# Attention start-up on one core: filler matmuls between the first heads' row scores, with clears and transposes reordered

## The chip, the cores and the metric

The kernel runs on one core of one Trainium2 chip. The metric is the device time of one execution in microseconds, the median of several runs; lower is better.

## The reference

32 heads of causal attention (4 batches of 8 heads, 576 positions, 64 columns per head) with a bias made of a running sum, and then two gated networks.

```python
scores = scale * np.matmul(q, k.transpose(0, 1, 3, 2))
cum = np.cumsum(np.maximum(s, 0.0), axis=-1)
bias = -(cum[:, :, :, None] - cum[:, :, None, :])
scores = np.where(causal, -1000000000.0, scores + np.minimum(bias, 0.0))
attn = np.exp(scores - np.max(scores, axis=-1, keepdims=True))
attn = attn / (np.sum(attn, axis=-1, keepdims=True) + 1e-09)
x = np.matmul(attn, v)            # then (2304, 512)
x = (1 / (1 + np.exp(-(x @ w_gate))) * (x @ w_val)) @ w_out
out = ((x @ w_a) * (x @ w_b)) @ w2_out
```

## The kernel before

The attention part takes the first fifth of the time and the two networks the rest. Everything is recorded as operations with a name, an engine, dependencies and a priority number. In the attention part a list scheduler (`emit(in_order=True)`) takes, among the operations whose dependencies have been taken, the one with the lowest number; so the numbers set the order of the instructions on each engine's queue, and each queue is then worked off strictly in that order, with semaphores between the engines. A transfer is issued by SP's, ACT's or GpSimd's queue and counts as an instruction of it.

One head i goes through these operations; the names are used below.

- `lqk` (L380, SP) loads the head's q and k. `hq1`, `hk1` (L532, L533, ACT) round them into the operand tile `o` (four of these tiles, used in turn; rows 0 to 63 are q and k, the rows behind hold the bias).
- The bias rows of `o` are filled by transfers: `sel` (L435 and L436, SP: two constant pieces), `rel` (L542, SP, from head 3 on), `relk` (L500 on SP for heads 0 to 2, L543 on GpSimd from head 3 on), and `relq` (L476, several queues, heads 0 to 2). Rows 64 to 127 of each `o` tile have to be cleared before: tile 0 at L390 (VectorE), tiles 1 and 2 by `ms` (L488, GpSimd), tile 3 by the first line of `more` (L399, VectorE).
- `S(i,0)` and `S(i,1)` (L557 and L562, TensorE) are the row scores in two halves, three matmuls and then one or two bf16 products that add the causal mask from `mkb` through the unit matrix `idb`. `mx(i,0)`, `mx(i,1)` (L570, VectorE) take their row maxima.
- `mT(i)` (L577, TensorE) transposes the maxima, `mc` (L579, ACT) copies them, `md` (L581, ACT's queue) sends them into `o`.
- `hk2`, `hq2` (L534, L535) send the rounded halves across, and `lok`, `loq` (L536, L538) take the low parts.
- `ST(i)` (L594 and L595, TensorE) are the transposed scores; they need `md(i)`, `lok(i)` and `loq(i)`. Then come the exponentials (L600, ACT), the causal clears (L616, GpSimd) and, by pairs of heads, the products with the values (L641) and the sums (L654).

`busy` (L410) is a run of products that nobody reads, TensorE's first work, 40 of them; it needs `mkb`, which ACT makes from GpSimd's `masks`. `more` clears tile 3 of `o` and eight small pieces of other tiles. The row scores of the first heads share one accumulator tile `g` for S(i,0): S(i+1,0) has to wait until mx(i,0) has read it.

The first of the networks' weight loads (L194, SP, 512 KB) stands on SP's queue between `rel(3)` and `sel(3)`:

```python
op(("more"), "DVE", 2.2, more, [], -149)
op(("rel", i), "SP", 0.5, lambda: ..., relst + done, t0 - 3 * HT + 0.05, lat=2.2)
```

A wait that follows from two writes of the same place is put in by the tile framework, in the order in which the operations are recorded, whether or not it is in an operation's list of dependencies.

Of the kernel before, what the change touches and what calls it, by code (L numbers as in the profile page):

```python
# [12 lines left out]
ALU = mybir.AluOpType  # L13
# [9 lines left out]
def f32(ap):  # L23
    return ap.bitcast(FP32)


class Schedule:
# [92 lines left out]
def attn_mlp_kernel(  # L120
# [14 lines left out]
    nc = tc.nc  # L135
# [3 lines left out]
    D = vt.shape[-1]  # L139
# [193 lines left out]
    def attention():  # L333
        with ExitStack() as c2:
# [16 lines left out]
            KB = R1 + 2  # L351
# [3 lines left out]
            CQ1, CK1 = 0, 640  # L355
# [6 lines left out]
            dn = tile1([128, QD], FP32, "dn")  # L362
# [4 lines left out]
            idb = tile1([128, 128], BF16, "idb")  # L367
            mkb = tile1([128, 448], BF16, "mkb")
# [3 lines left out]
            o_t = [tile1([128, CK1 + S], F32R, f"o{i}") for i in range(NO)]  # L372
            p_t = [tile1([128, 2 * S], F32R, f"o2_{i}") for i in range(3)]
            rel = tile1([128, 2, S], F32R, "rel")
# [31 lines left out]
            def busy():  # L406

                ps = sc.get("F", "busy")
                for _ in range(NBUSY):
                    nc.tensor.matmul(out=ps[:, 0:256], lhsT=idb, rhs=mkb[:, 192:448], start=True, stop=True)  # L410

            def selector():

                nc.gpsimd.memset(sel, 1.0)
                nc.gpsimd.affine_select(sel, sel, [[1, S]], ALU.is_ge, 0.0, base=0, channel_multiplier=-SR)
                nc.gpsimd.affine_select(sel, sel, [[-1, S]], ALU.is_ge, 0.0, base=SR - 1, channel_multiplier=SR)
# [17 lines left out]
            def selectors(o):  # L434
# [3 lines left out]
            sc = Schedule({  # L438
                "g": [psum1("ps_g", 1024)],
                "E": [psum1("ps_e", 1024)],  # L440
                "F": [psum1("ps_f")],
                "t": [psum1("ps_t")],
                "px": [psum1("ps_x", 1024)],
                "raw": list(raw_t),
                "u": [0],
                "W": wslot[:2],
                "stg": stg,
            })
            op = sc.op
# [33 lines left out]

            op("s", "SP", 0.5, load_s, [], -300, lat=2.3)
            op("selc", "Pool", 1.9, selector, [], -300)
            op("masks", "Pool", 0.9, masks, ["selc"], -280)
            for j in range(1, 3):
                op(("ms", j), "Pool", 1.2, lambda j=j: nc.gpsimd.memset(f32(o_t[j][D:2 * D]), 0.0), ["masks"], -270)  # L488
            op("pads", "DVE", 0.6, pads, [], -249)
            op("more", "DVE", 2.2, more, [], -149)  # L490
            op("mkb", "ACT", 0.7, masks_b, ["masks"], -280)
            op("mkc", "ACT", 0.2, masks_c, ["mkb"], -279)
            op("busy", "PE", 8.0, busy, ["mkb"], -270, acq=("F", "busy"), rel=("F", "busy"))
# [5 lines left out]
            for i in range(3):  # L499
                op(("relk", i), "SP", 0.65, lambda i=i: nc.sync.dma_start(  # L500
                    out=f32(o_t[i][D:R1, CK1:CK1 + S]), in_=f32(rel[i:NR * BH:BH])), ["sums"] + [("ms", i)] * (i > 0), -210 + i, lat=2.2)
# [6 lines left out]
            relst = ["relz"] + [("rels", c) for c in range(NR)]  # L508

            HT = 6.1  # L510
            NBUSY = 40
            WLATE = HT

            def head(i):
                b, h = divmod(i, H)  # L520
                t0 = HT * i
                o, o2, r, pt = o_t[i % NO], p_t[i % 3], r_t[i % NR2], pt_t[i % NPT]
                nm, mr = nm_t[i % 4], mr_t[i % 3]
                k1, q1, k2, q2 = o[:, CK1:CK1 + S], o[:, CQ1:CQ1 + S], o2[:, S:2 * S], o2[:, 0:S]
                up, dn = slice(0, D), slice(D, 2 * D)
                done = [("ST", i - NO, c) for c in range(NC)] + [("S", i - NO, g) for g in range(2)]
                done2 = [("ST", i - 3, c) for c in range(NC)]

                if i >= NR2:
# [4 lines left out]
                op(("hk2", i), "ACT", 0.7, lambda: nc.scalar.dma_start(out=f32(k2[dn]), in_=f32(k1[up])), [("hk1", i)] + done2, (-209.8, -209.6, -8.55)[i] if i < NR2 else t0 - 2 * HT + 0.35)  # L534
                op(("hq2", i), "SP", 0.5, lambda: nc.sync.dma_start(out=f32(q2[up]), in_=f32(q1[up])), [("hq1", i)] + done2, (-208.5, -207.5, -206)[i] if i < NR2 else t0 - 2 * HT + 0.1)  # L535
                op(("lok", i), "DVE", 0.9, lambda: nc.vector.tensor_tensor(  # L536
                    out=k2[up], in0=r[dn], in1=f32(k2[dn]), op=ALU.subtract), [("hk2", i)], (-8.7, -8.3)[i] if i < 2 else t0 - HT - 0.3)
                op(("loq", i), "DVE" if i < 2 else "Pool", 0.9 if i < 2 else 1.4, lambda: (nc.vector if i < 2 else nc.gpsimd).tensor_tensor(  # L538
                    out=q2[dn], in0=r[up], in1=f32(q1[up]), op=ALU.subtract), [("hq1", i)] + done2, -151 + 2 * i if i < 2 else t0 - HT + 1.45)

# [7 lines left out]
                for g, cs in ((0, (3, 2, 0)), (1, (1, 4))):  # L548
# [26 lines left out]
                       first_at[g] if first_at and first_at[g] else t0 + (3.5 - 2 * HT, -HT)[g], acq=to)  # L575
                    op(("mx", i, g), "DVE", (1.4, 1.1)[g], maxima, [("S", i, g), ("mT", i - 4), "pads"], (first_at[g] or 6.1) + 0.05 if first_at else t0 + (4.3 - 2 * HT, 0.7 - HT)[g], rel=to)
                op(("mT", i), "PE", 0.15, lambda: nc.tensor.transpose(sc.get("t", ("m", i))[0:NC, 0:128], nm[:, 0:NC], idf),  # L577
                   [("mx", i, 0), ("mx", i, 1), "masks"], (-8.7, -8.4)[i] if i < 2 else t0 - HT + 3.4, acq=("t", ("m", i)))
                op(("mc", i), "ACT", 0.25, lambda: nc.scalar.copy(out=mr, in_=sc.get("t", ("m", i))[0:NC, 0:128]),  # L579
                   [("mT", i), ("md", i - 3)], (-8.7, -8.4)[i] + 0.05 if i < 2 else t0 - HT + 3.55, rel=("t", ("m", i)))  # L580
                op(("md", i), "ACT", 0.4, lambda: nc.scalar.dma_start(  # L581
                    out=f32(o[KB:KB + 1, CQ1:CQ1 + 640]), in_=f32(mr)), [("mc", i)] + done, (-8.7, -8.4)[i] + 0.06 if i < 2 else t0 - HT + (3.93, 5.21)[i % 2], lat=2.2)


                tiles = {0: ("E", (i, 0)), 1: ("E", (i, 0)), 2: ("F", (i, 0)), 3: ("F", (i, 0)), 4: ("t", ("p", i))}
# [109 lines left out]
            for e, (ld, ab, *dv) in enumerate(LOADS):  # L695
                n, m = e // 2, e % 2
                prio = HT * ld + (0.5 if e > 2 else 0)
                last = convert(sc, n, m, [("S", max(int(ld) - 1, 0), 0)], prio,
                               at=[HT * ab + 1.2 - prio] + [HT * dv[k] - 0.15 + y - prio for k, y in ((0, 0), (0, 0.01), (1, 0), (2, 0))])
# [8 lines left out]
            done = [("xd", j) for j in range(H)]  # L708
# [302 lines left out]
```

## Time and profile before

| what | value |
|---|---|
| median of 3 runs | 1040.98 us (1038.46 to 1041.43) |
| the profiled execution | 1043.03 us |
| its span | 1041.3 us, so 1.7 us lie around it |
| TensorE busy in the span | 1011.0 us, 97% |
| TensorE's granted clock over the span | 0.992 of full |

The span is the time between the first and the last instruction of the profiled execution. A busy TensorE is one that has a matmul in it, at whichever clock. The granted clock is 1.0 at 2.4 GHz and 0.5 at 1.2 GHz; before the first change that the profiler saw it is shown as 1.0.

### The profile page before, as it was taken

Reading aid. Unit: us, or ns where it says so; the run is one execution under the profiler, and the core shown is the slowest. Engines: PE = TensorE matmul, PEld = TensorE weight load, DVE = VectorE, ACT = ScalarE, POOL = GpSimd, SP = SyncE. Lnnn points to the kernel's source line nnn. Section 1 sums busy time; section 2 is a strip of 40 time slices with the busy share of each in tenths; the row PEclk is TensorE's granted clock in tenths of the full one; section 3 lists DMA queues with packets and bytes.
Section 4 is the critical chain, followed back from the end, with each engine's and each line's share of the span. In section 5 each row is a group of like instructions: output and inputs, shape, how many; then the busy total and the mean of one; then the engine's idle time right before and its main releaser. Section 6 shows DMA issues by size and latency. Waiting matters only on the chain.

```text
span 1041.3 us, 17117 instructions
## 1 busy us (share of the span) xinstructions
PE 1011.0 (97%) x6160; PEld 914.1 (88%) x6160; DVE 694.4 (67%) x1146; ACT 466.8 (45%) x891; POOL 388.1 (37%) x388
## 2 busy tenths in 40 slices
PE   6999999999999999999999999999999999999998
PEld 5777666789999999998888899999999999888886
DVE  7787778779689665669855238967876567933222
ACT  3566666655455444545334225343433333432221
POOL 5568687652366333433300013245532342400000
PEclk7999999999999999999999999999999999999999
DMA  5667777441243321446553442123432244544333
GB/s 147 172 160 200 206 206 170 129 147 58 101 131 111 128 99 69 145 159 231 178 171 109 122 128 83 59 102 127 128 109 94 92 153 160 196 138 133 111 107 101
DMA packets 93586, 139.76 MB, mean 134 GB/s; under 512 B 16215, under 2 KB 54863, under 8 KB 93502
## 3 DMA queue, kind: packets, MB, share of 16 engines
q1 hardware_dynamic: 89234, 133.03, 41.1%
q10 hardware_dynamic: 2988, 4.95, 1.8%
q0 software_dynamic: 1280, 0.70, 0.3%
q8 instruction: 48, 0.79, 0.3%
q14 instruction: 36, 0.29, 0.1%
HBM read 85.53 MB, written 33.45 MB: 114 GB/s over the span
## 4 chain that ended last, share of the span: by engine, by line
PE 79%; DVE 11%; DMA 5%; issue 2%; POOL 1%; ACT 1%; SPq 0%; ACTq 0%; DVEq 0%; POOLq 0%
PE ps L291 23%; PE ps L290 23%; PE ps L292 23%; PE ps_x L641 2%; DVE nm L570 2%; PE ps_g L557 2%; DMA rb<-rr_d 1%; PE ps_e L594 1%; DVE s L824 1%; PE ps_e L595 1%; DVE o L536 1%; DVE u L218 1%; PE ps_x L654 1%; DVE x_sb L324 1%; DMA r<-in_qk_dram 1%
## 5 line engine op out<-in xcount | busy, mean ns | idle before, releaser
L290 PE MATMUL ps<-rg,wk 128*128 128x384 f32 (+2 forms) x1128 | 381.9, 339 | 4.0 <-DVE s L824 4.0
L292 PE MATMUL ps<-rg,wk 128*128 128x384 f32 (+2 forms) x1128 | 381.0, 338 | 0.0
L290 PEld LDWEIGHTS ps<-rg,wk 128*128 128x128 f32 x1128 | 211.8, 188 | 10.1 <-DVE s L824 5.4
L292 PEld LDWEIGHTS ps<-rg,wk 128*128 128x128 f32 x1128 | 211.8, 188 | 3.7
L824 DVE TENSOR_TENSOR s<-ps,s 128x384 f32<-128x384 f32 x216 | 118.8, 552 | 113.7 <-PE ps L292 65.0
L291 PE MATMUL ps<-x_sb,wk 128*128 128x384 f32 x576 | 192.6, 334 | 0.8 <-DVE x_sb L324 0.8
L291 PE MATMUL ps<-rg,wk 128*128 128x384 f32 (+2 forms) x552 | 188.5, 342 | 0.0
L837 POOL TENSOR_TENSOR hs<-s,s 128x384 f32<-128x384 f32 x72 | 90.1, 1252 | 262.0 <-issue 79.5
L821 ACT COPY s<-ps 128x384 f32<-128x384 f32 x216 | 103.5, 481 | 178.2 <-PE ps L292 177.0
L268 POOL TENSOR_TENSOR wk<-raw,wk 128x512 fp32r<-128x512 f32 x96 | 126.1, 1342 | 149.8 <-PE ps L292 102.8
L904 DVE TENSOR_TENSOR rg<-rg 128x512 fp32r<-128x512 f32 (+1 forms) x120 | 80.7, 678 | 110.9 <-ACT rg L903 106.9
L903 ACT CAST rg<-rg 128x512 fp32r<-128x512 f32 (+1 forms) x120 | 68.4, 578 | 146.7 <-DMA rg<-hd 105.3
L291 PEld LDWEIGHTS ps<-x_sb,wk 128*128 128x128 f32 x576 | 108.1, 188 | 1.2 <-DVE x_sb L324 1.1
L291 PEld LDWEIGHTS ps<-rg,wk 128*128 128x128 f32 x552 | 103.7, 188 | 3.7
L570 DVE TENSOR_REDUCE nm<-ps_g 128x1 f32<-128x512 f32 (+4 forms) x154 | 74.2, 531 | 35.1 <-PE ps_g L562 34.9
L290 PE MATMUL ps<-rg,rg 128*128 128x512 f32 (+1 forms) x228 | 86.1, 378 | 0.0
L291 PE MATMUL ps<-rg,rg 128*128 128x512 f32 (+1 forms) x228 | 86.1, 378 | 0.0
L292 PE MATMUL ps<-rg,rg 128*128 128x512 f32 (+1 forms) x228 | 86.1, 378 | 0.0
L215 ACT ACTIVATE mag<-raw 128x512 f32<-128x512 f32 x72 | 48.5, 674 | 56.3 <-DVE raw L223 28.5
L616 POOL TENSOR_SCALAR_AFFINE_SELECT pt<-pt 128x256 f32<-128x256 f32 (+1 forms) x96 | 45.4, 496 | 56.4 <-ACT pt L600 49.9
L220 DVE SCALAR_TENSOR_TENSOR raw<-raw,u 128x512 int32<-128x512 int32 x72 | 61.6, 856 | 4.1
L832 ACT ACTIVATE s<-s 128x384 f32<-128x384 f32 x72 | 37.8, 526 | 55.5 <-DVE s L824 55.4
(120 smaller groups left out, 1519.4 us busy)
## 6 DMA issues: line engine op xcount, KB each, us to landing
hd<-hs SPq DMA_DIRECT2D x72, 384.0 KB
rg<-hd SPq DMA_DIRECT2D x72, 256.0 KB
raw<-in_moe_w_out_dram SPq DMA_DIRECT2D x24, 512.0 KB
r<-in_qk_dram SPq DMA_DIRECT2D x32, 288.0 KB
rg<-hd SPq DMA_DIRECT2D x72, 128.0 KB
raw<-in_moe_w_gate_dram SPq DMA_DIRECT2D x12, 512.0 KB
raw<-in_moe_w_val_dram SPq DMA_DIRECT2D x12, 512.0 KB
raw<-in_moe_w_a_dram SPq DMA_DIRECT2D x12, 512.0 KB
```

What stands on the lines that cost most here:

```text
L215: ("ACT", 0.6, lambda: nc.scalar.activation(out=mag, in_=parts(n, m)[1].bitcast(FP32), func=ACTF.Abs)),
L220: ("DVE", 0.65, lambda: nc.vector.scalar_tensor_tensor(out=parts(n, m)[1], in0=parts(n, m)[0], scalar=29, in1=u, op0=ALU.logical_shift_rig ...
L268: return lambda: nc.gpsimd.tensor_tensor(out=wcols(n, a, w, 1), in0=src(), in1=f32(wcols(n, a, w, 0)), op=ALU.subtract)
L290: nc.tensor.matmul(out=outp, lhsT=wh, rhs=xh, start=start and e == 0, stop=False, skip_group_check=True)
L291: nc.tensor.matmul(out=outp, lhsT=wh, rhs=xl, start=False, stop=False, skip_group_check=True)
L292: nc.tensor.matmul(out=outp, lhsT=wl, rhs=xh, start=False, stop=stop and e == n - 1, skip_group_check=True)
L570: nc.vector.tensor_reduce(out=nm[0:n, c:c + 1], in_=ps[0:n, p0:p0 + nk], axis=AX.X, op=ALU.max)
L821: op((x,) + key, "ACT", ACT_P, lambda x=x: nc.scalar.copy(out=s(x), in_=bank("X")), [P(p)], end(p) - 10, acq=("s", key + (x,)))
L824: return lambda: nc.vector.tensor_tensor(out=s(x), in0=bank(b_), in1=s(x), op=ALU.add)
L837: op(("h2",) + key, "Pool", PTT, lambda: nc.gpsimd.tensor_tensor(out=half(1), in0=s("s4"), in1=s("s2"), op=ALU.mult), [("c22",) + key, (g[ ...
L903: op(("hh",) + key, "ACT", 0.17 + 0.00083 * N, lambda hs=hs, N=N: nc.scalar.copy(out=hs()[:, 0, 0:N], in_=f32(hs()[:, 1, 0:N])), [("hl",) ...
L904: op(("ho",) + key, "DVE", 0.157 + 0.00104 * N, lambda hs=hs, N=N: nc.vector.tensor_tensor(out=hs()[:, 1, 0:N], in0=f32(hs()[:, 1, 0:N]), ...
```

## The change

There are five edits, all in the attention part's start-up.

- `fill`: two new groups of products that nobody reads, 16 behind S(0,1) and 8 behind S(1,1), into the upper half of the tile `t` that also takes the transposed maxima.
- `mT(0)`, with its `mc` and `md`, gets a lower number and so stands ahead of S(1,0) on TensorE; `lok(0)` comes ahead of mx(1,0) on VectorE.
- `more` goes from -149 to -8.2, that is, from ahead of the first maxima to behind lok(1).
- GpSimd clears tile 1 of `o` ahead of `masks` instead of behind it.
- `busy` has 36 products instead of 40.

```diff
+            def fill(key, n):
+
+                ps = sc.get("t", key)
+                for _ in range(n):
+                    nc.tensor.matmul(out=ps[:, 256:512], lhsT=idb, rhs=mkb[:, 192:448], start=True, stop=True)
+
...
-            op("masks", "Pool", 0.9, masks, ["selc"], -280)
+            op("masks", "Pool", 0.9, masks, [("ms", 1)], -280)
             for j in range(1, 3):
-                op(("ms", j), "Pool", 1.2, lambda j=j: nc.gpsimd.memset(f32(o_t[j][D:2 * D]), 0.0), ["masks"], -270)
+                op(("ms", j), "Pool", 1.2, lambda j=j: nc.gpsimd.memset(f32(o_t[j][D:2 * D]), 0.0), ["selc"] if j == 1 else ["masks"], -270)
...
-            op("more", "DVE", 2.2, more, [], -149)
+            op("more", "DVE", 2.2, more, [], -8.2)
...
-            NBUSY = 40
+            NBUSY = 36
...
+            fills = {("f", 0): (16, -8.83), ("f", 1): (8, -8.55)}
+            for k, (n, at) in fills.items():
+                op(k, "PE", 0.1 * n, lambda k=k, n=n: fill(k, n), ["mkb"], at, acq=("t", k), rel=("t", k))
...
-                    out=k2[up], in0=r[dn], in1=f32(k2[dn]), op=ALU.subtract), [("hk2", i)], (-8.7, -8.3)[i] if i < 2 else t0 - HT - 0.3)
+                    out=k2[up], in0=r[dn], in1=f32(k2[dn]), op=ALU.subtract), [("hk2", i)], (-8.84, -8.3)[i] if i < 2 else t0 - HT - 0.3)
...
-                   [("mx", i, 0), ("mx", i, 1), "masks"], (-8.7, -8.4)[i] if i < 2 else t0 - HT + 3.4, acq=("t", ("m", i)))
+                   [("mx", i, 0), ("mx", i, 1), "masks"], (-8.82, -8.4)[i] if i < 2 else t0 - HT + 3.4, acq=("t", ("m", i)))
```

On TensorE, from the end of S(0,1) (`ps_x`) to the start of S(1,0) (`ps_g`) and mT(0) (`ps_t<-idf,nm`), before:

```order
L557 MATMUL ps_x<-o_198 128x256
L562 LDWEIGHTS idb
L562 MATMUL ps_x<-mkb,idb 128x320
L557 MATMUL ps_g<-o_202 128x512
L557 MATMUL ps_g<-o_202 128x384
L557 MATMUL ps_g<-o_202 128x128
...
L577 MATMUL ps_t<-idf,nm_162 5x128
L557 MATMUL ps_x<-o_202 128x256
```

and now (line numbers are 10 higher from here on; the two rows of L416 stand 16 times):

```order
L567 MATMUL ps_x<-o_198 128x256
L572 LDWEIGHTS idb
L572 MATMUL ps_x<-mkb,idb 128x320
L416 LDWEIGHTS idb
L416 MATMUL ps_t<-mkb,idb 128x256
...
L587 MATMUL ps_t<-idf,nm_162 5x128
L567 MATMUL ps_g<-o_202 128x512
```

mT(0) has moved from behind S(1,0) to ahead of it, with 16 products in front of it; 8 more stand between S(1,1) and S(2,0), which is not shown.

On VectorE, from loq(0) (L538, then L548) to the maxima of head 2, before (tile 0 to 3 of `o` are o_198, o_202, o_206, o_210; the maxima of heads 0, 1, 2 go to nm_162, nm_166, nm_170):

```order
L538 TENSOR_TENSOR o_0_214<-r_110,o_198 64x576
L399 MEMSET o_210 64x1216
...
L404 MEMSET pt_146 64x64
L538 TENSOR_TENSOR o_1_218<-r_114,o_202 64x576
L570 TENSOR_REDUCE nm_162<-ps_g 128x1 x3
...
L570 TENSOR_REDUCE nm_166<-ps_g 128x1 x3
L536 TENSOR_TENSOR o_0_214<-r_110,o_0_214 64x576
```

and now:

```order
L548 TENSOR_TENSOR o_1_218<-r_114,o_202 64x576
L580 TENSOR_REDUCE nm_162<-ps_g 128x1 x3
...
L546 TENSOR_TENSOR o_0_214<-r_110,o_0_214 64x576
L580 TENSOR_REDUCE nm_166<-ps_g 128x1 x3
...
L580 TENSOR_REDUCE nm_170<-ps_g 128x1 x3
L546 TENSOR_TENSOR o_1_218<-r_114,o_1_218 64x576
L399 MEMSET o_210 64x1216
...
L404 MEMSET pt_146 64x64
L546 TENSOR_TENSOR o_2_222<-r_118,o_2_222 64x576
```

The clear of tile 3 (o_210) and the small clears have moved from ahead of head 0's maxima to behind lok(1) (which writes o_1_218), between the two halves of head 2's maxima.

On SP's queue, from lqk(3) to lqk(4), before, with the semaphores that each row waits for (DMAHW and DMASW are transfers, DVE is VectorE):

```order
L380 DMA r_110<-in_qk_dram 128x576 [waits DMAHW5_49,DVE_49]
L542 DMA o_210<-relq_d 3x576 [waits DMASW7_49,DMAHW3_49,DMASW2_49,DMAHW7_49,DMASW1_49,DMASW0_49]
L194 DMA raw_64<-in_moe_w_gate_dram 128x4x256 [waits DMAHW0_49]
L435 DMA o_210<-pt_138 8x1x576 [waits DMAHW1_49]
L436 DMA o_210<-pt_142 3x576 [waits DMAHW2_49]
L380 DMA r_114<-in_qk_dram 128x576 [waits DMAHW4_49,DVE_49]
```

and now:

```order
L380 DMA r_110<-in_qk_dram 128x576 [waits DMAHW5_49,DMAHW4_49,DVE_49]
L552 DMA o_210<-relq_d 3x576 [waits DMASW7_49,DMASW2_49,DMAHW3_49,DMASW1_49,DMAHW7_49,DMASW0_49,DVE_49]
L194 DMA raw_64<-in_moe_w_gate_dram 128x4x256 [waits DMAHW1_49]
L441 DMA o_210<-pt_138 8x1x576 [waits DMAHW2_49]
L442 DMA o_210<-pt_142 3x576 [waits DMAHW4_49]
L380 DMA r_114<-in_qk_dram 128x576 [waits DMAHW5_49]
```

The order on SP is the same, but rel(3) (L542, now L552) has a wait for VectorE that it did not have; the weight load and sel(3) stand behind it.

## Rows read from the trace of the kernel before

**Rows 1.** The page: busy time by engine, and TensorE's clock in 40 slices.

```profile
PE 1011.0 (97%) x6160; PEld 914.1 (88%) x6160; DVE 694.4 (67%) x1146; ACT 466.8 (45%) x891; POOL 388.1 (37%) x388
PEclk7999999999999999999999999999999999999999
```

**Rows 2.** Stretches of the span: length, busy time by engine, granted clock, DMA share, GB/s.

```profile
14.00:31.00 17.00, 14.93 (x54) 11.80 (x54) 9.89 (x20) 6.96 (x14) 5.68 (x12) 0.50 0.72 195
31.00:60.00 29.00, 26.76 (x247) 20.05 (x248) 23.33 (x42) 17.79 (x36) 16.01 (x24) 1.00 0.59 156
232.00:1041.30 809.30, 803.00 (x4289) 752.65 (x4287) 514.93 (x816) 326.13 (x617) 232.75 (x180) 1.00 0.38 123
```

**Rows 3.** The chain that ended last, 24 to 43 us: start, us, what.

```profile
24.95 0.37 PE ps_t L577
25.32 1.08 PE ps_g L557 x3
...
30.70 0.31 PE ps_g L562
...
39.31 0.46 PE ps_g L557 x3
...
42.09 0.15 PE ps_g L562
```

**Rows 4.** Timeline of TensorE: start, us, instruction, and the idle time before it.

```profile
4.45 5.82 PE L410 MATMUL ps_f<-mkb,idb 128*128 128x256 bf16 x40 [4.45 <-ACT mkb L428]
11.74 0.71 PE L557 MATMUL ps_g<-o 128*128 128x512 f32 x3 [1.47 <-ACT o L532]
12.85 0.31 PE L562 MATMUL ps_x<-mkb,idb 128*128 128x320 bf16 x1
14.22 1.19 PE L557 MATMUL ps_g<-o 128*128 128x512 f32 x3 [1.06 <-DMA o<-o]
15.55 0.42 PE L577 MATMUL ps_t<-idf,nm 128*5 128x128 f32 x1
```

**Rows 5.** Timeline of VectorE, 10 to 25 us.

```profile
10.12 1.07 DVE L399 MEMSET o<- 64x1216 f32 x1 [0.20 <-issue]
12.66 1.35 DVE L570 TENSOR_REDUCE nm<-ps_g 128x1 f32<-128x512 f32 x3
13.93 1.07 DVE L570 TENSOR_REDUCE nm<-ps_x 128x1 f32<-128x256 f32 x2
17.18 0.75 DVE L536 TENSOR_TENSOR o<-r,o 64x576 fp32r<-64x576 f32 x1
18.93 1.35 DVE L570 TENSOR_REDUCE nm<-ps_g 128x1 f32<-128x512 f32 x3
20.19 1.42 DVE L536 TENSOR_TENSOR o<-r,o 64x576 fp32r<-64x576 f32 x2
23.73 1.08 DVE L570 TENSOR_REDUCE nm<-ps_x 128x1 f32<-128x256 f32 x2 [2.11 <-PE ps_x L562]
```

**Rows 6.** Timeline of SP's and ACT's queues, 18 to 25 us: issues of transfers.

```profile
18.92 0.26 SPq L542 DMA_DIRECT2D o<-relq_d  x1
19.23 0.40 SPq L194 DMA_DIRECT2D raw<-in_moe_w_gate_dram  x1
19.77 0.71 ACTq L581 DMA_DIRECT2D o<-mr  x1
20.47 0.74 SPq L436 DMA_DIRECT2D o<-pt  x1
24.71 0.39 SPq L384 DMA_DIRECT2D vx<-in_vm_dram  x1
```

**Rows 7.** Waits of SP's queue, 15 to 27 us: total, times, longest.

```profile
SPq L384 <- DMA o<-mr: 3.0, 1, 3.0
```

**Rows 8.** Line 476, 9 to 12.5 us: issue to landing of its small transfers.

```profile
DMA to landing us min/median/max: 1.7/2.2/3.0
```

**Rows 9.** Timeline of GpSimd: `ms(1)` and `ms(2)`.

```profile
4.08 2.47 POOL L488 MEMSET o<- 64x1216 f32 x2
```

More of the change, by code (lines that the diff above doesn't have):

```diff
@@ L577, in head @@
                 op(("mT", i), "PE", 0.15, lambda: nc.tensor.transpose(sc.get("t", ("m", i))[0:NC, 0:128], nm[:, 0:NC], idf),
-                   [("mx", i, 0), ("mx", i, 1), "masks"], (-8.7, -8.4)[i] if i < 2 else t0 - HT + 3.4, acq=("t", ("m", i)))
+                   [("mx", i, 0), ("mx", i, 1), "masks"], (-8.82, -8.4)[i] if i < 2 else t0 - HT + 3.4, acq=("t", ("m", i)))
                 op(("mc", i), "ACT", 0.25, lambda: nc.scalar.copy(out=mr, in_=sc.get("t", ("m", i))[0:NC, 0:128]),
-                   [("mT", i), ("md", i - 3)], (-8.7, -8.4)[i] + 0.05 if i < 2 else t0 - HT + 3.55, rel=("t", ("m", i)))
+                   [("mT", i), ("md", i - 3)], (-8.82, -8.4)[i] + 0.005 if i < 2 else t0 - HT + 3.55, rel=("t", ("m", i)))
                 op(("md", i), "ACT", 0.4, lambda: nc.scalar.dma_start(
-                    out=f32(o[KB:KB + 1, CQ1:CQ1 + 640]), in_=f32(mr)), [("mc", i)] + done, (-8.7, -8.4)[i] + 0.06 if i < 2 else t0 - HT + (3.93, 5.21)[i % 2], lat=2.2)
+                    out=f32(o[KB:KB + 1, CQ1:CQ1 + 640]), in_=f32(mr)), [("mc", i)] + done, (-8.82, -8.4)[i] + 0.006 if i < 2 else t0 - HT + (3.93, 5.21)[i % 2], lat=2.2)
                 tiles = {0: ("E", (i, 0)), 1: ("E", (i, 0)), 2: ("F", (i, 0)), 3: ("F", (i, 0)), 4: ("t", ("p", i))}
```

## The prediction, on record before the result

> **What bounds the kernel now.** I read the page first: TensorE is busy 97% of the span, and its clock is full everywhere but in the first slice [rows 1]. By stages, the two networks have no room: 803 us busy of 809 from 232 us on [rows 2]. After 31 us the attention part, too, is mostly TensorE's, 26.8 us busy of 29 [rows 2]. So whatever the change wins or loses, it does so before 31 us, and what it moves there is passed on to the end, since nothing behind has the slack to take it up. From 14 to 31 us TensorE is granted half its clock while it is busy 14.9 of 17 us [rows 2].
>
> Second, the chain. It runs through S(3,0) at 25.32, ST(1) and S(3,1), which ends at 31.01: 5.7 us at half clock [rows 3]. The same sequence two heads later, at full clock, runs from 39.31 to 42.24: 2.9 us [rows 3]. That is what the clock is worth here, some 2.8 us. What TensorE did before the clock fell at 14: 40 products up to 10.27, nothing for 1.47 us, S(0,0) and S(0,1) up to 13.16, nothing for 1.06 us [rows 4].
>
> Third, SP's queue. rel(3) goes out at 18.92, the 512 KB weight load right behind it at 19.23, and the second piece of sel(3) at 20.47 [rows 6]. The next transfer, at 24.71, had waited 3.0 us for a small one, md(1), issued at 19.77 [rows 6, 7]: a transfer of 2.5 KB took up to 4.9 us because it went out behind the weight load. S(3,0) needs sel(3), which went out later still, and it began at 25.2, right behind mT(2) [rows 3]. So sel(3) landed by 25.2, and hardly before 24.7: S(3,0) had almost no slack against it.
>
> **The change part by part.** *Masks behind one clear, 36 products.* A clear by GpSimd takes half of 2.47 us [rows 9], so `mkb` and the first product come 1.2 us later, at 5.6. 36 products at the mean of 5.82/40 = 0.146 us take 5.2 us and end at 10.9, before S(0,0) at 11.74, which waits for its own transfers [rows 4]. Price nothing. If all 36 ran at half clock (0.21 us each; 40 in 5.82 us were part half, part full) they would end at 13.2, 1.4 us too late; that is the upper bound.
>
> *`more` out of the way.* It filled VectorE from 10.12 to 12.0, and loq(1) came behind it, but mx(0,0) at 12.66 began as S(0,0) ended (11.74 and 0.9 us) [rows 4, 5]. Price and gain there: nothing.
>
> *The fillers.* Full-clock products take about half of 0.21, 0.107 us: 16 are 1.7 us, 13.16 to 14.9. mT(0) can't start before mx(0,1) ends at 15.0 [rows 5], so they are hidden by VectorE, and the gap in TensorE's work shrinks to 0.2 us. At half clock they would be 3.4 us and push mT(0) 1.5 us back; I take the full clock.
>
> *mT(0) sooner.* 15.1 instead of 15.55 [rows 4]; S(1,0) goes from 14.22 to 15.25, but at full clock it takes 0.9 us and ends at 16.15, 0.4 us behind its old end. md(0) gains 0.5 us.
>
> *VectorE's row, which now decides.* mx(0,1) ends at 15.0, lok(0) 0.75 to 15.8; mx(1,0) waits for S(1,0): 16.15 to 17.5; mx(1,1) 1.07 to 18.6; S(2,0) behind its tile's release and the 8 fillers, 17.6 to 18.5; mx(2,0) 18.6 to 19.95; lok(1) half of 1.42, to 20.7; and only then the clear of tile 3, 1.07 us, **to 21.8** [rows 5]. Before, that clear was done at 11.2. The other clears (0.75 us up to 12.0 before) and lok(2) follow, so mx(2,1) runs 23.2 to 24.3 against 23.73 to 24.8: 0.5 us gained, and mT(2) at 24.4.
>
> *The new wait.* rel(3), relk(3) and sel(3) write into the rows of tile 3 that the clear writes, so they go behind it; the order shows a wait for VectorE on rel(3) that was not there. rel(3) moves from 18.92 to 21.85, **2.9 us later**, and behind it on SP's queue stand the weight load, sel(3) and lqk(4). The weight load and lqk(4) have time (SP stood idle until 24.71 anyway [rows 6, 7]). sel(3)'s second piece goes out at 23.4. Its way to landing has two bounds: 2.2 us, the median of small transfers with nothing large ahead [rows 8], so 25.6; and 4.9 us, that of md(1), so 28.3. It has the same weight load ahead of it as before, when it took at most 25.2 - 20.47 = 4.7 us, so I take the upper end, landing at 27.9. S(3,0) then starts at 27.9 instead of 25.2: **+2.7 us**. The Trainium skill's "DMA: Bandwidth & Descriptors", section on queues, rings and completion order, says that each DMA engine takes a queue's descriptors in ring order and that a completion lands only after the engine's earlier writes, across its queues; by that rule too sel(3) can't overtake the load, and md(1), on another queue, agrees with it.
>
> *The clock at 27.9.* TensorE has S(2,1) done at 21.3 (ST(0) at full clock from 18.7) and then only mT(2) until 27.9. It fell at 14 after less idle time than that, so S(3,0), ST(1) and S(3,1) run at half again, as before: 5.7 us, to 33.6 against 31.0. Bounds: nothing returned, or all of 2.8 us. I take nothing, because at half clock 14.9 us busy of 17 did not bring it back [rows 2]. The skill's "TensorE: Matmul & The Clock Gate", Part 1, says that the throttle is released by sustained activity; by it the unbroken run from 27.9 could be freed on the way, and part of the 2.8 us returned. The rows of 14 to 31 don't show that at once.
>
> **The sum.** 0 (masks, products, fillers) + 2.7 (S(3,0)) - 0 (clock) = +2.7 us on the chain. The profiled execution took 1043.03 us, so 1045.7 in its terms; it lay 2.05 us above the median of the runs, so the median is 1040.98 + 2.7 = **1043.7 us**.
>
> **The rivals.** *Held, but the clock makes up for it (1041).* S(3,0) at 27.9 but 2.9 us instead of 5.7: S(3,1) ends at 30.8 against 31.0, no change. Or sel(3) lands at 25.6 by its lower bound: +0.4. For it: the fillers close both gaps ahead of the fall at 14. Against: 6 us nearly idle ahead of 27.9, and md(1)'s 4.9 us. This is also where the change would do nothing. Some 1039.8 to 1042.2.
>
> *Faster (1037.4 to 1039.5).* sel(3) lands before mT(2), S(3,0) starts at 24.5 and the clock stays full: 24.5 + 2.9 = 27.4 against 31.0, -3.6 us, so 1037.4; with half of the clock's worth 1039. It decides itself at one place: sel(3) must land by 24.5, 1.1 us after it is issued, or rel(3) not wait for the clear. The shortest landing I see is 1.7 us [rows 8], so that needs the clear some 1 us or more earlier than I sum.
>
> *Slower still (1045.3 to 1046.5).* The clock stays half past S(3,1), so that the next head's 2.8 us are paid in full or half as well (TensorE has a gap again while mx(3,1) runs, 1.1 us), or the 36 products run into S(0,0) (up to 1.4 us) and shift VectorE's whole row.
>
> **How the numbers follow.** Chances: main 0.50 (its own range 1042.3 to 1045.3), no change 0.24, faster 0.14, slower still 0.12. A measurement tells about 0.3%, 3.1 us, from no change: below 1037.9 lies 0.06 (the good end of "faster"), above 1044.1 lie 0.20 of the main case and 0.12, and 0.62 are between. The range 1039.0 to 1045.5 leaves out a good part of "faster" and most of "slower still", some 2 in 10.
>
> **What would show it.** The first product at 5.6 and the last filler of the first group before 15.0: the masks and fillers are free. Full clock from 11 to 21: the fillers do what they can. The clear of tile 3 ending near 21.8, rel(3)'s issue right behind it, an SP wait on VectorE of some 2 to 3 us in the list of waits: the new wait. S(3,0) at 27.9 with a transfer, not VectorE, as what ended TensorE's idle time. Half clock around 28 to 33. I am wrong if S(3,0) starts before 26, or if the clock is full at 28.

## The result, and the profile after

The changed kernel takes 1045.01 us (median of 7 runs, 1043.93 to 1049.04), the kernel before 1040.03 in the same comparison (7 runs, 1038.24 to 1043.39): a ratio of 1.0056, 95% interval 1.0038 to 1.0075. It is 5.0 us slower, where +2.7 was forecast and "within 0.3%" was held likelier than "slower".

The page answers [rows 1]: TensorE is as busy as before, and its clock has no long low stretch at the start.

```profile
PE 1011.3 (97%) x6180; PEld 914.3 (87%) x6180; DVE 691.2 (66%) x1146; ACT 467.2 (45%) x891; POOL 386.7 (37%) x388
PEclk9899999999999999999999999999999999999999
```

The same stretches as in [rows 2], and a shorter one (length, busy time of PE, PEld, DVE, ACT and POOL, granted clock, DMA share, GB/s):

```profile
14.00:31.00 17.00, 11.00 (x70) 8.44 (x69) 11.54 (x27) 4.96 (x10) 4.82 (x8) 0.85 0.59 158
26.20:32.80 6.60, 4.33 (x15) 3.60 (x16) 2.04 (x5) 1.96 (x4) 1.78 (x2) 0.50 0.89 244
31.00:60.00 29.00, 26.67 (x242) 20.65 (x241) 21.70 (x40) 17.38 (x35) 16.56 (x25) 0.97 0.60 159
```

From 14 to 31 us the mean clock is 0.85 instead of 0.50 and TensorE is busy for 11.0 us instead of 14.9. Busy time at the higher clock is worth more, but S(3,1), done at 31.0 before, is done at 33.9 now, so the time that the clock gave, and more, is idle time. Where it lies shows in the timeline of TensorE (start, us, instruction, the idle time before it and what ended it), to be held against [rows 4]:

```profile
6.63 6.90 PE L410 MATMUL ps_f<-mkb,idb 128*128 128x256 bf16 x36 [6.63 <-ACT mkb L434]
13.29 0.71 PE L567 MATMUL ps_g<-o 128*128 128x512 f32 x3
...
14.55 1.91 PE L416 MATMUL ps_t<-mkb,idb 128*128 128x256 bf16 x16
16.61 0.27 PE L587 MATMUL ps_t<-idf,nm 128*5 128x128 f32 x1
16.92 0.70 PE L567 MATMUL ps_g<-o 128*128 128x512 f32 x3
...
26.37 0.37 PE L587 MATMUL ps_t<-idf,nm 128*5 128x128 f32 x1 [3.58 <-DVE nm L580]
...
28.84 1.19 PE L567 MATMUL ps_g<-o 128*128 128x512 f32 x3 [2.10 <-DMA o<-pt]
...
33.10 0.63 PE L567 MATMUL ps_g<-o 128*128 128x256 f32 x3
33.57 0.31 PE L572 MATMUL ps_g<-mkb,idb 128*128 128x320 bf16 x1
```

The fillers do close the two gaps (16 products from 14.55, mT(0) right behind mx(0,1)). But between S(2,1), done at 22.8, and S(3,0) at 28.84 TensorE has one short transpose, and a transfer, not VectorE, ends the wait. S(3,1) ends at 33.9. The chain that ended last says which transfer (start, us, what), against [rows 3]:

```profile
22.54 1.08 DVE o L399
23.64 0.26 SPq L552
23.95 0.40 SPq L194
24.41 0.74 SPq L441
25.20 3.40 DMA o<-pt
28.59 0.25 issue
28.84 1.19 PE ps_g L567 x3
```

The chain is the clear of tile 3, then rel(3), the weight load and the two pieces of sel(3) in SP's order, the flight of the second piece (its time from issue to landing), and S(3,0). SP's list of waits names the first link, where [rows 7] had 3.0 us for another line:

```profile
SPq L552 <- DVE o L399: 5.7, 1, 5.7
```

That execution took 1049.04 us, the longest of the seven; a second profile of the changed kernel, from one of 1044.61, shows what of it repeats (below). Of all executions in this document one lies far off, 3539.19 us, of early_all: it is left out of that kernel's interval, and the median without it is 1039.81.

### The profile page after: what moved, and what is told of

The parts are those of the page before. It is cut to its first block, busy times and chain, and to the rows that moved or that the text cites. A ratio compares the mean times of both kernels' runs of the same rounds, so it can differ in the third digit from the quotient of the medians.

```text
span 1047.0 us, 17156 instructions
## 1 busy us (share of the span) xinstructions
PE 1011.3 (97%) x6180; PEld 914.3 (87%) x6180; DVE 691.2 (66%) x1146; ACT 467.2 (45%) x891; POOL 386.7 (37%) x388
## 4 chain that ended last, share of the span: by engine, by line
PE 81%; DVE 8%; DMA 5%; issue 2%; POOL 1%; ACT 1%; SPq 1%; ACTq 0%; POOLq 0%; DVEq 0%
PE ps L291 23%; PE ps L290 23%; PE ps L292 23%; PE ps_x L651 3%; DMA o<-o 2%; PE ps_g L567 2%; DVE nm L580 2%; PE ps_e L604 1%; PE ps_e L605 1%; PE ps_x L664 1%; DVE s L834 1%; DMA hd<-hs 1%; POOL hs L847 1%; DVE u L218 1%; DVE rg L324 1%
## 5 line engine op out<-in xcount | busy, mean ns | idle before, releaser
L215 ACT ACTIVATE mag<-raw 128x512 f32<-128x512 f32 x72 | 48.6, 675 | 55.8 <-DVE raw L223 25.3
L626 POOL TENSOR_SCALAR_AFFINE_SELECT pt<-pt 128x256 f32<-128x256 f32 (+1 forms) x96 | 43.1, 472 | 54.5 <-ACT pt L610 52.3
```

Source lines behind the costliest of these rows:

```text
L215: ("ACT", 0.6, lambda: nc.scalar.activation(out=mag, in_=parts(n, m)[1].bitcast(FP32), func=ACTF.Abs)),
```

## The experiments

Times are medians of 7 to 12 runs; the kernel before, run beside each, lay at 1040.1 to 1040.8. Single runs of it spread from 1035.1 to 1045.2, so differences of under 2 us between two kernels tell little, and the intervals are given where they decide.

**Which part does it.** *clears_early*: the change, with the clears back ahead of head 0's maxima.

```diff
-            op("more", "DVE", 2.2, more, [], -8.2)
+            op("more", "DVE", 2.2, more, [], -149)
```

> The changed kernel with all of the clears of `more` back at -149, ahead of head 0's maxima; nothing else undone. Theory A (the clear of tile 3 holds rel(3), sel(3) and so S(3,0)): S(3,0) starts at 25 to 26.5 us instead of 28.8, released by VectorE through mT(2) and not by a transfer, and the time falls by 2.5 to 4 us from the changed kernel's 1045.0, to 1041 to 1042.5. Rival B (the masks behind a clear, so that the 36 products run into S(0,0), is most of the loss): at most 1 us is won, 1044 or more.

Measured: 1039.82, ratio to before 1.0010 (0.9993 to 1.0027). The whole loss is gone, more than was expected of it. Timeline of VectorE and TensorE:

```profile
9.94 1.07 DVE L399 MEMSET o<- 64x1216 f32 x1 [0.20 <-issue]
24.19 0.70 PE L567 MATMUL ps_g<-o 128*128 128x512 f32 x3
```

S(3,0) is 4.65 us earlier than in the first profile of the changed kernel (4.1 than in the second) and runs at full clock (0.70 us for its first product group, not 1.19).

*masks_first*: the change, with `masks` ahead of both GpSimd clears again, the VectorE clears still late.

```diff
-            op("masks", "Pool", 0.9, masks, [("ms", 1)], -280)
+            op("masks", "Pool", 0.9, masks, ["selc"], -280)
...
-                op(("ms", j), "Pool", 1.2, lambda j=j: nc.gpsimd.memset(f32(o_t[j][D:2 * D]), 0.0), ["selc"] if j == 1 else ["masks"], -270)
+                op(("ms", j), "Pool", 1.2, lambda j=j: nc.gpsimd.memset(f32(o_t[j][D:2 * D]), 0.0), ["masks"], -270)
```

> The changed kernel with GpSimd's masks ahead of both clears again; `more` stays late. Theory A: S(0,0) starts at 11.5 instead of 13.3, VectorE's row and with it the clear of tile 3 end 1.5 us sooner, S(3,0) at 27.3; 1 to 2 us won, 1043 to 1044, still slower than before by 3. Rival B: at least 3 us won, 1042 or less.

Measured: 1045.58 (1.0027 to 1.0063): nothing won, where 1 to 2 us were expected. In its profile S(0,0) is back at 11.69 and S(3,0) starts at 27.09, but at half clock that lasts to 33 us all the same, so ST(2) begins at 34.89, where the two profiles of the changed kernel have 35.04 and 35.91.

*both_back*: both of these undone, so that the fillers, mT(0) and lok(0) sooner, and the 36 products stay.

> The changed kernel with both undone: what is left are the fillers, mT(0) and lok(0) sooner and 36 products. Theory A with the masks as the second part: all of the loss is gone, 1037.5 to 1040.5, at or below before. Rival C (the fillers themselves or mT(0) ahead of S(1,0) cost something): 1 us or more above before, 1041 and more.

Measured: 1040.40, 0.9999 (0.9985 to 1.0013). The fillers and the sooner transpose are worth nothing that can be measured.

*tile3_early*: the change, with the clear of tile 3 alone taken out of `more` and put at -149; the small clears stay late.

```diff
+            op("clear3", "DVE", 1.1, clear3, [], -149)
-            op("more", "DVE", 2.2, more, [], -8.2)
+            op("more", "DVE", 1.1, more, ["clear3"], -8.2)
```

> The changed kernel in which only the clear of tile 3 goes back to -149; the eight small clears stay behind lok(1). Theory A: the same as with all clears back (within 0.7 us of it), since only tile 3's clear has a transfer waiting for it. Rival D (it is VectorE's time between the two halves of head 2's maxima that costs, through mT(2)): more than 1 us above the kernel with all clears back.

Measured: 1040.76, 1.0011 (0.9996 to 1.0026). That is 0.9 us above clears_early, just between the two expectations, with intervals that overlap almost wholly. So it is this one clear, not the small ones (seven, by the trace: L400 once, L402 twice and L404 four times; not eight).

*only_clears_late*: the kernel before with this one number changed, from -149 to -8.2, and nothing else.

> The kernel before with one part of the change alone: the clears of tile 3 and of the small pieces go behind lok(1). By the theory that this part makes the whole loss, the clear of tile 3 ends at 21 to 22 us, rel(3) behind it, S(3,0) starts at 27 to 29 us, TensorE's clock is half there, and the time is that of the changed kernel, 1044 to 1046. If the other four edits had a share in the loss, it comes out clearly below, 1041 to 1043; if they make up for some of it, above 1047.

Measured: 1045.60, 1.0049 (1.0029 to 1.0070), the time of the whole change. Timeline of TensorE, and the stretch of half clock behind it:

```profile
26.88 1.19 PE L557 MATMUL ps_g<-o 128*128 128x512 f32 x3 [2.18 <-DMA o<-pt]
```

```profile
23.00:39.90 16.90, 12.13 (x44) 9.86 (x44) 9.16 (x16) 7.24 (x14) 6.84 (x13) 0.50 0.67 188
```

Without the other four edits S(3,0) starts 1.4 to 2 us sooner than in the changed kernel. That comes from the masks and not from the missing fillers, since masks_first, which has the fillers and S(0,0) at 11.69, starts S(3,0) at 27.09. But here the clock stays half until 40 us, in masks_first until 33: what the earlier start gives, the clock takes.

**The transfer behind the weight load.** *sel3_first*: the change, with sel(3) ahead of the weight load on SP's queue; the clears stay late.

```diff
-                op(("sel", j), "SP", 1.3, lambda j=j: selectors(o_t[j]), ["selc"] + [("ms", j) if j < 3 else "more"] * (j > 0), (-260, -257, -208, 0.5)[j], lat=2.2)
+                op(("sel", j), "SP", 1.3, lambda j=j: selectors(o_t[j]), ["selc"] + [("ms", j) if j < 3 else "more"] * (j > 0), (-260, -257, -208, 0.1)[j], lat=2.2)
```

> The changed kernel with one more edit: on SP's queue both pieces of sel(3) stand ahead of the 512 KB weight load (priority 0.1 instead of 0.5); the clear of tile 3 is as late as in the change. Theory A1 (the late clear moves sel(3) back and the weight load ahead of it adds to its way): sel(3) lands 2 to 2.5 us after its issue instead of 3.4, S(3,0) starts at about 27 instead of 28.8, 1 to 2 us won, 1043 to 1044. Rival (the weight load has no part in it): S(3,0) within 0.5 us of 28.8 and the time unchanged at 1045.

Measured: 1041.57, 1.0015 (1.0001 to 1.0028): 3.4 us of the 5 are back with the clear still late (21.24 to 22.31), more than expected. Timeline of SP's queue and TensorE:

```profile
6.66 5.57 PE L410 MATMUL ps_f<-mkb,idb 128*128 128x256 bf16 x36 [6.66 <-ACT mkb L434]
11.99 0.71 PE L567 MATMUL ps_g<-o 128*128 128x512 f32 x3
...
23.45 0.74 SPq L442 DMA_DIRECT2D o<-pt  x1
24.23 0.42 SPq L194 DMA_DIRECT2D raw<-in_moe_w_gate_dram  x1
...
25.78 1.19 PE L567 MATMUL ps_g<-o 128*128 128x512 f32 x3 [0.34 <-DMA o<-pt]
```

The second piece of sel(3) has landed 2.1 us after its issue, against the 3.40 us of the chain above, and the 2.10 us of idle time ahead of S(3,0) became 0.34. Not all of the 3.1 us at S(3,0) are the queue's: the 36 products took 5.57 us in this execution instead of 6.90, so S(0,0) and the clear came 1.3 us sooner, by luck. In sel3_one_fill below, where S(0,0) starts at 13.34, S(3,0) gains 1.75.

**The clock in the gap.** *gap_filled*: the change, with 30 products that nobody reads behind S(2,1) and 18 behind mT(2), in accumulator tile `g`.

```diff
...
+            op(("f", 2), "PE", 3.0, lambda: fill(("f", 2), 30, "g", 0), [("S", 2, 1)], 8.0, acq=("g", ("f", 2)), rel=("g", ("f", 2)))
+            op(("f", 3), "PE", 1.8, lambda: fill(("f", 3), 18, "g", 0), [("mT", 2)], 9.55, acq=("g", ("f", 3)), rel=("g", ("f", 3)))
```

> The changed kernel with two more groups of products that nobody reads, 30 behind S(2,1) and 18 behind mT(2), in the stretch in which TensorE waits for sel(3); all waits stay. Theory A2 (a part of the loss is the clock, which falls in that stretch): S(3,0) still starts at about 28.8, but at full clock, S(3,1) ends 2 us sooner, 1042.5 to 1043.5. Rival (the loss is the wait alone, the clock's share is taken up by later waits): 1045 as before.

Measured: 1043.97 (1.0016 to 1.0051), in two clusters of runs, 1040.5 to 1043.1 and 1044.9 to 1046.3. Timeline of TensorE:

```profile
21.90 3.44 PE L416 MATMUL ps_g<-mkb,idb 128*128 128x256 bf16 x30
25.64 0.27 PE L589 MATMUL ps_t<-idf,nm 128*5 128x128 f32 x1 [0.29 <-DVE nm L582]
25.74 2.13 PE L416 MATMUL ps_g<-mkb,idb 128*128 128x256 bf16 x18
27.96 0.70 PE L569 MATMUL ps_g<-o 128*128 128x512 f32 x3
```

S(3,0) starts as the 18 products end, as late as predicted for the change (27.96), but at full clock; ST(3) begins at 38.92 instead of 42.69 and 40.81 in the two profiles of the changed kernel. The median gains only 1.0 us, and its interval overlaps with the change's.

*sel3_and_gap*: both cures together.

> The changed kernel with both cures at once, the clears still late: sel(3) ahead of the weight load, and 48 products that nobody reads around mT(2). By the theory that the loss has two terms, S(3,0) late behind sel(3) and the clock that falls in the gap ahead of it, nothing or up to 1 us is left of it: S(3,0) at 25 to 26, full clock, 1040 to 1041.5. If the clock has no share, it comes out as with sel(3) first alone, 1041.6, or later, since the products now hold S(3,0) up (they end at some 27.8 us, as in the kernel with the products alone): 1042 to 1044.

Measured: 1043.45 (1.0010 to 1.0046): a miss. The 18 products run until S(3,0) and hold it at 27.94, so that sel(3), there by about 26.4 (its issue at 24.33 and the 2.1 us of sel3_first, an estimate), wins nothing.

*sel3_one_fill*: the same without those 18.

> As with both cures, but without the 18 products behind mT(2), which held S(3,0) up until 27.94: sel(3) ahead of the weight load, the clears still late, and 30 products between S(2,1) and mT(2). S(3,0) should start at 25.8 to 26.5, as with sel(3) first alone, but at full clock. If the half clock behind S(3,0) costs time of its own, the median comes out 0.5 to 1.5 us below that of sel(3) first alone (1041.57), at 1040 to 1041. If the clock falls and returns somewhere else anyway, so that the total is the same, 1041 to 1042.

Measured: 1046.14 (1.0029 to 1.0065): the largest miss, 4.6 us slower than without the 30 products, though S(3,0) starts at 27.09 and the clock is full until 33. Its timeline on ACT and TensorE shows the next wait:

```profile
30.19 0.67 ACT L543 CAST o<-r 64x576 fp32r<-64x576 f32 x1 [3.21 <-DMA r<-in_qk_dram]
31.46 1.01 ACT L611 ACTIVATE pt<-ps_e 128x1024 f32<-128x1024 f32 x1
33.11 0.38 PE L588 MATMUL ps_t<-idf,nm 128*5 128x128 f32 x1 [2.86 <-ACT pt L611]
```

ACT's queue stands for 3.21 us before hq1(4) (L543), which waits for lqk(4), the 288 KB transfer that SP issued at 26.07, right behind the weight load at 25.59. The exponentials of head 1 (L611) stand behind it on ACT, and mT(3) waits for them, because it takes the tile `t` that they read. TensorE is idle from 30.2 to 33.1, and its clock falls there: `33.10:36.30` is granted 0.50.

**lqk(4), the second place behind rel(3).** *load_last*: the change, with the weight load behind sel(3) and lqk(4). *load_last_fill*: the same with the 30 products of sel3_one_fill. *load_before*: the weight load ahead of rel(3) instead (-0.2 in place of 0.66; the number, times 6.1, is the load's place in the order).

```diff
-            LOADS = [(0.02, 2, 2.5, 3, 4), (2, 4, 5, 6, 7), (5, 8, 10, 11, 12), (12, 14, 15, 16, 17), (14, 17, 20, 21, 22), (21, 23, 24, 25, 27)]
+            LOADS = [(0.66, 2, 2.5, 3, 4), (2, 4, 5, 6, 7), (5, 8, 10, 11, 12), (12, 14, 15, 16, 17), (14, 17, 20, 21, 22), (21, 23, 24, 25, 27)]
```

> The changed kernel, clears still late, with the weight load behind sel(3) and lqk(4) on SP's queue. If lqk(4) is the second place that the wait on rel(3) makes late: S(3,0) at about 26, ACT's rounding of head 4 at 27 to 28 (28.8 with sel(3) first alone), the exponentials of head 1 right behind, and the time 0.5 to 1.5 us below that of sel(3) first alone (1041.6): 1040 to 1041. If lqk(4) has time, 1041.3 to 1042. If the weight load, later now, is itself late for the first weights' conversion, above 1042.

> The kernel with 30 products between S(2,1) and mT(2) and the weight load behind both sel(3) and lqk(4). If lqk(4) made the loss of sel3_one_fill (1046.1), it goes back to that of the kernel without the products, 1040 to 1041.5. If the products themselves do harm (the gap in TensorE's work comes later and the clock falls where nothing covers it, at 33 us instead of 23), it stays above 1043.

> The changed kernel, clears still late, with the weight load ahead of rel(3) on SP's queue, where it doesn't wait for the clear: issued at about 17 us. sel(3) and lqk(4) are then late by the clear alone, with nothing large ahead of them: S(3,0) at about 26, and 1040 to 1041.5. Against it: the load now runs beside the small transfers of heads 0 to 2 (md(0), md(1), hk2(2)), of which md(0) and md(1) gate the first transposed scores; if they are held up by 2 us or more, 1043 to 1046.

Measured: load_last_fill 1041.56 (1.0004 to 1.0042), load_last 1043.92 (1.0019 to 1.0048), load_before 1044.72 (1.0026 to 1.0054). For the first, timeline of ACT and TensorE:

```profile
28.40 0.67 ACT L543 CAST o<-r 64x576 fp32r<-64x576 f32 x1 [1.51 <-DMA r<-in_qk_dram]
...
29.67 1.01 ACT L611 ACTIVATE pt<-ps_e 128x1024 f32<-128x1024 f32 x1
31.42 0.27 PE L588 MATMUL ps_t<-idf,nm 128*5 128x128 f32 x1 [1.26 <-DVE nm L581]
```

With lqk(4) ahead of the load the same products do no harm: mT(3) comes 1.7 us earlier and waits for VectorE's maxima again, the clock is full all through the attention part, and 4.6 us are back in the medians (the intervals still overlap). At half clock lqk(4) isn't the bound. In load_last the exponentials wait for TensorE:

```profile
27.15 0.67 ACT L542 CAST o<-r 64x576 fp32r<-64x576 f32 x1 [1.46 <-DMA r<-in_qk_dram]
29.27 1.02 ACT L610 ACTIVATE pt<-ps_e 128x1024 f32<-128x1024 f32 x1 [0.76 <-PE ps_e L605]
```

Its start is the same as that of sel3_first (ST(3) at 38.70 and 38.81), so by this stage it should have come out at 1041.6 too. It came out above 1042, where a weight load that is late for its conversion was expected to put it; but the first step of that conversion on ACT (L215) starts at 31.20, and at 31.70 in sel3_first, so the profile shows no such lateness there. load_before lies in its rival's range, but not for the rival's reason: ST(0), which waits for md(0), starts 7.0 us behind S(0,0), as in sel3_first and the changed kernel. Its start is later than sel3_first's: S(3,0) by 0.6 us (26.38), the end of S(3,1) by 1.0 (32.01 and 30.99), and ST(3) by 2.1 (40.89), after a conversion step on VectorE (L216) ahead of mx(4,0) took 1.63 us instead of 0.43.

*masks_load_last*: load_last with the masks first on GpSimd.

> The changed kernel, clears still late, with the masks ahead of both clears on GpSimd and the weight load behind sel(3) and lqk(4). S(0,0) at 11.7 us. If the masks' late start is what holds the kernel with the load last at 1043.9, this one comes out at 1040.5 to 1042. If the masks have no share, 1043 to 1044.5, and what holds it stays open.

Measured: 1041.91 (0.9999 to 1.0035). By the medians that would be a share of the masks of 2 us once the transfers are cured, but the intervals overlap, and the profiles don't show it: S(0,0) starts at 11.74, and at 11.94 in load_last's, and ST(3) comes later here (40.01 and 38.70).

**A version that beats both?** *all_good*: both_back with sel(3) ahead of the load and 20 products between S(2,1) and mT(2). *early_load_last*: both_back with the load behind sel(3) and lqk(4). *early_all*: that with the 20 products.

> Clears early and masks first as in the kernel before, with the change's fillers and mT(0) sooner, sel(3) ahead of the weight load, and 20 more products between S(2,1) and mT(2). Theory: S(3,0) starts at about 23.8, always at full clock: 1036.5 to 1038.5, 2 to 4 us below the kernel before. Rival (the kernel before is at full clock there in most of its executions anyway): 1039.5 to 1040.5, no change.

> The kernel with the clears early, the masks first, the fillers and mT(0) ahead as in the change, and the weight load behind sel(3) and lqk(4). With the clears early sel(3) was already just in time, and sel(3) first won nothing measurable there; ACT's rounding of head 4 waited 2.25 us for lqk(4) until 26.39, and the exponentials of head 1 stood behind it. If that is the bound in this kernel, and so in the one before as well, 1038 to 1039.5; if TensorE's clock and the next heads swallow it, 1040.

> The kernel with early clears, masks first, the weight load behind sel(3) and lqk(4), and 20 more products between S(2,1) and mT(2). If the gap ahead of mT(2) and its clock are what is left in the kernel before, the clock stays full up to 34 us and it comes out 1 to 2 us below the kernel before: 1038 to 1039.5. If the clock only falls in a later gap, 1040, as with sel(3) first and the same products.

Measured: 1040.06 (0.9982 to 1.0009), 1040.22 (0.9971 to 1.0004) and 1039.86 (0.9979 to 1.0008). None is told from the kernel before. S(3,0) starts at 23.35 to 23.74 in them, and the clock falls one gap later, ahead of mT(3) (early_all: mT(3) at 29.00 after 2.09 us idle), so that ST(3) stands at 37.1 to 37.2, as in the second profile of the kernel before.

**Second profiles.** The kernel before and the changed kernel, profiled once more.

> The kernel before, profiled once more. Theory A3 (the profiled execution on which the sum rested was one of its slower ones): the clock is full for a larger part of 14 to 31 us, ST(3) starts at 36 to 38 us instead of 39.7, and the span is 1037 to 1039 us. Rival: half clock from 14 to 31 again and a span of 1041.

> The changed kernel once more, for its profile. If the second loss, between the heads 15 and 22 (90 to 125 us), belongs to the change, the transposed scores of head 22 start 5 us behind those in the first profile of before again; if it was that execution's own, 2 to 3.5 us, as much as at head 3. S(3,0) at 27 to 29 us and half clock from about 26 to 33 us either way.

The kernel before, one execution of 1041.12 us, TensorE's timeline, the stretch of half clock, and the flight of sel(3)'s second piece in the chain that ended last:

```profile
24.80 1.03 PE L557 MATMUL ps_g<-o 128*128 128x512 f32 x3 [1.11 <-DMA o<-pt]
...
29.24 0.31 PE L562 MATMUL ps_g<-mkb,idb 128*128 128x320 bf16 x1
```

```profile
25.10:28.30 3.20, 3.20 (x13) 2.73 (x12) 2.01 (x4) 1.40 (x3) 0.95 (x1) 0.50 0.72 181
```

```profile
20.39 4.17 DMA o<-pt
```

The half clock from 14 to 31 us in [rows 2] is not in every execution: here it is half only from 25.0 to 28.4, S(3,1) ends at 29.55 instead of 31.01, and ST(3) starts at 37.35 instead of 39.71. And sel(3) already ends TensorE's wait there: the slack against it was none. The span is 1039.4, a little more than expected. The changed kernel, one execution of 1044.61 us:

```profile
28.32 1.19 PE L567 MATMUL ps_g<-o 128*128 128x512 f32 x3 [2.04 <-DMA o<-pt]
```

Start, transfer and half clock (24.8 to 31.6) repeat. The second loss of the first profile, between heads 15 and 22 with half clock from 118 to 122 us, doesn't: head 22's transposed scores start at 151.8 instead of 156.5 (in the second profile of the kernel before, at 149.0). Second profile against second profile the change costs 3.5 us at S(3,0) (24.80 to 28.32), 3.5 at ST(3) (37.35 to 40.81), and 3.2 in the spans (1039.4 to 1042.6); first against first 3.6, 3.0 and 5.7.

All kernels, starts in us as their profiles show them:

| kernel | clear of tile 3 | S(0,0) | S(3,0) | ST(3) | median |
|---|---|---|---|---|---|
| before (first, second profile) | early | 11.74, 11.70 | 25.22, 24.80 | 39.71, 37.35 | 1040.0 to 1040.8 |
| clears_early | early | 12.74 | 24.19 | 35.15 | 1039.82 |
| both_back | early | 11.74 | 24.19 | 36.74 | 1040.40 |
| tile3_early | early | 13.29 | 25.12 | 38.64 | 1040.76 |
| all_good | early | 11.70 | 23.50 | 37.23 | 1040.06 |
| early_load_last | early | 11.71 | 23.35 | 37.18 | 1040.22 |
| early_all | early | 11.71 | 23.74 | 37.11 | 1039.86 |
| after (first, second profile) | late | 13.29, 12.80 | 28.84, 28.32 | 42.69, 40.81 | 1045.01 |
| only_clears_late | late | 11.73 | 26.88 | 43.25 | 1045.60 |
| masks_first | late | 11.69 | 27.09 | 41.59 | 1045.58 |
| sel3_first | late | 11.99 | 25.78 | 38.81 | 1041.57 |
| gap_filled | late | 12.55 | 27.96 | 38.92 | 1043.97 |
| sel3_and_gap | late | 12.87 | 27.94 | 39.50 | 1043.45 |
| sel3_one_fill | late | 13.34 | 27.09 | 41.11 | 1046.14 |
| load_last | late | 11.94 | 25.68 | 38.70 | 1043.92 |
| load_before | late | 12.72 | 26.38 | 40.89 | 1044.72 |
| load_last_fill | late | 13.23 | 26.98 | 38.08 | 1041.56 |
| masks_load_last | late | 11.74 | 25.48 | 40.01 | 1041.91 |

The line between the groups is the place of one clear of 1.07 us: no kernel that has it early is above 1040.8, none that has it late below 1041.5.

## Why the prediction was right and wrong

**The mechanism was right.** The clear behind lok(1), the new wait of rel(3), sel(3) behind the weight load, S(3,0) released by it: each link is in the chain above, tile3_early shows that undoing this clear suffices to undo the loss, and only_clears_late that it suffices to make it. How much of the time the weight load's place makes is not settled. Of the kernels with the late clear and sel(3) not behind the load, sel3_first wins 3.4 us of the median, load_last 1.1 and load_before 0.3. The Trainium skill's "DMA: Bandwidth & Descriptors", section on queues, rings and completion order, was cited for sel(3) not overtaking the load; the same section says that completion is not first in, first out for an issuing engine, so the rule reaches only the DMA engines that both transfers use. The runs agree in kind: 2.97 to 4.17 us of flight behind the load in the chains of six profiles, 2.03 to 2.08 in four with the load elsewhere on the queue; when the load itself landed, no row shows.

**The fillers and the sooner mT(0): nothing.** Right, 0.9999 in both_back.

**S(3,0): +2.7.** This is the step that failed, mis-sized: S(3,0) comes 3.6 us later in the first profiles (25.22 to 28.84) and 3.5 in the second (24.80 to 28.32). What made it so is the term put at nothing, the masks and the 36 products. The first product came at 6.63, not 5.6, the 36 took 6.90 us instead of 5.2, and they ran into S(0,0): 13.29 instead of 11.74, past the +1.4 held as the upper bound and chosen against (12.80 in the second profile). That moved VectorE's whole row: the clear ended at 23.6 (23.15 in the second profile), not 21.8, and rel(3) went out 4.7 and 4.3 us later, not 2.9. Luck hid part of it: sel(3)'s second piece, sent at 25.20 and not at 23.4, was 3.40 us on its way (3.35 in the second profile) instead of the 4.5 allowed, which gave 1.1 us back. masks_first takes this term out of S(3,0) (27.09), but not out of the median (1045.58): the clock is half over all of S(3,0), ST(1) and S(3,1) there, 5.8 us. The Trainium skill's "TensorE: Matmul & The Clock Gate", Part 1, has a remark that the number of slow products at a kernel's start varies from run to run; the 36 products agree, with 6.90 and 6.12 us in the two profiles of the changed kernel and 5.57 in sel3_first.

**The clock: 0, "as before".** On balance nothing contradicts the 0, but its working did not hold. Half clock lies behind the gap as said (26.2 to 32.8), but S(3,0) to the end of S(3,1) took 5.0 us, and 4.7 in the second profile, not 5.7; that S(3,1) was done at 33.9, where 33.6 was summed, is the later start and the shorter sequence cancelling, so luck. In the kernel before the 5.7 us were those of one execution with a granted clock of 0.992; the second profile, of one with 0.998, has 4.75 and ends at 29.55. Neither is the usual one. Of the 148 executions of the kernel before that were run beside the experiments, 17 were granted 0.992 or less, 19 were granted 0.998 or more, and the median is 0.995. The seven of the changed kernel have 0.993 to 0.997, median 0.996, so it spends no more time at half clock. At the same granted clock, 0.995 to 0.997, the loss stays: a median of 1040.2 us before (83 executions) and 1045.2 after (6). Two other kernels with the late clear have less: only_clears_late a median of 0.993, masks_first 0.994.

**lqk(4) "has time".** Right as long as S(3,0) is the bound, wrong once S(3,0) comes sooner and the clock is full: sel3_one_fill shows it as the next wait on the same queue.

**The rivals.** "Slower still" named the second mechanism, the products that run into S(0,0); the time, 1045.0, stayed at the upper end of the main case's own range (1042.3 to 1045.3). "Faster" needed the clear 1 us sooner than summed, and it came 1.4 to 1.8 later. "Held, but the clock makes up for it" has the start of gap_filled, where the clock is full, and even that is 3.2 us slower than before.

**Open.** The start-up costs 3.5 us by the second profiles, the medians differ by 5.0 (4.0 to 7.8 by the interval), and no run shows where the rest lies. 8 of the 20 profiles have further spells of half clock much later, seven of the twelve with the late clear and one of the eight with the early one, for instance load_last:

```profile
125.80:129.00 3.20, 3.13 (x12) 2.70 (x13) 1.43 (x4) 1.65 (x4) 2.32 (x2) 0.50 0.86 261
```

This execution took 3.6 us more than the profiled one of sel3_first (1043.61 and 1040.00) from the same start, and lost them late: its transposed scores of head 15 start 1.4 us ahead of the other's (107.43 and 108.81), those of head 22 1.35 us behind (151.66 and 150.31), with this spell between them, and 2.2 us more are lost behind head 31, around a second spell at 224 to 229 us. What sets such spells no run shows, and 20 profiles are too few to tell whether a kernel's start makes them more frequent. What the clock in the gap is worth by itself is settled only roughly too: 1.0 us by gap_filled, with intervals that overlap.

## What to carry to other kernels

An operation that is moved out of the way takes its readers with it: look for what writes the same place, on which queue it waits, and everything that stands behind it there, up to the second and third transfer, not only the first. A small transfer that gates TensorE belongs ahead of a large one that has time. And before pricing a stage from one profile, compare that execution's time and granted clock with those of the other executions: 1043.03 us at 0.992 was not the usual one here, and neither was the second profile's 0.998.

## What the runs showed of the hardware

GpSimd's select on 128x128 (L429) took 1.11 us beside VectorE's scan, and 0.29 us in the kernel before, where the scan came later, at 5.54. Timelines of VectorE and GpSimd in the changed kernel:

```profile
4.61 1.36 DVE L471 TENSOR_TENSOR_SCAN pt<-pt,pt 128x576 f32<-128x576 f32 x1
```

```profile
4.94 1.11 POOL L429 TENSOR_SCALAR_AFFINE_SELECT pt<-pt 128x128 f32<-128x128 f32 x1
```

The same select in the kernel before, timeline of GpSimd:

```profile
3.57 0.29 POOL L423 TENSOR_SCALAR_AFFINE_SELECT pt<-pt 128x128 f32<-128x128 f32 x1
```

Beside the scan it ends within 0.1 us of it, in all eleven profiles with this order on GpSimd (in the second profile of the changed kernel it is the other select, L426, with 1.26 us); in the nine with the masks first, both selects take 0.29 us. That is 0.8 of the 1 us by which the first product came later than summed. The Trainium skill's "GPSIMD Engine Reference", key points, says that GpSimd shares its interfaces to SBUF with VectorE, with contention where a VectorE instruction has two inputs there; the scan has two, and the trace agrees.
